# Zipformer block on one core: splitting the last 416-token chunk of the second batch into 256 and 160 tokens whose attention takes both pairs of heads in one exponential

## The chip, the core and the metric

One core of a Trainium2 chip. The metric is the device time of one execution in microseconds (us), the median of several runs. Timed runs take turns with runs of the kernel before on the same chip. "Ratio" always means the mean time of one kernel's fast runs over the mean time of the other's fast runs of the same rounds, so it is not quite the ratio of the medians quoted; intervals are 95%. Several chips were used, so times are compared within one job only.

## The reference, cut to what matters

Two sequences of 4000 tokens, width 144, four heads of 36, feed-forward width 576, everything in bf16.

```python
def reference(x, ...):
    x = x + 0.5 * silu(ln(x) @ w_ff1a) @ w_ff1b          # feed-forward 1
    q, k, v = split(ln(x) @ w_qkv)
    p = softmax(q @ k.T * Dh ** -0.5)                     # 4000 x 4000, per head and batch
    x = x + (p @ v) @ w_o
    a, b = split(ln(x) @ w_pw1)
    h = a * sigmoid(b)                                    # GLU
    x = x + silu(depthwise_conv5(h, dw)) @ w_pw2          # needs the two neighbour tokens on each side
    x = x + 0.5 * silu(ln(x) @ w_ff2a) @ w_ff2b           # feed-forward 2
    return ln(x)
```

## The kernel before

Python code generates the instructions one by one and orders them with a model of the engines' times (a list scheduler); each engine then runs its list in order. Each batch is cut into seven chunks of 512 tokens and one of 416: chunks 0 to 7 and 8 to 15.

```python
    CPB = -(-T // CH)                       # 8 chunks a batch, CH = 512
    def nc_(c):
        return min(CH, T - c % CPB * CH)    # 512, the last 416
```

Attention runs in groups: one chunk and one pair of heads. A group has 31 tiles of 128 keys; the last 32 keys are one more tile in the first group of each chunk, for all four heads. For a tile, TensorE makes the scores of both heads of the pair (four 64x64 pieces side by side), ScalarE takes one exponential over both (1024 columns, or 832 in the last chunk), TensorE multiplies by the values. VectorE computes the exponential of some tiles by a polynomial.

```python
    groups = [(b, qc, p) for b in range(Bsz) for qc in range(CPB) for p in range(2)]
    # cut
        for hh in range(2):                                          # emit_S: the scores of tile n
            bk = 2 * (n % 2) + hh
            s_mm(gi, kt, hh, PSV[:, bk, 0:m], [("ps", bk)], 0.0535)
    # cut
        exps[n] = op("act", "activation", PT[:, n % NPT, :, 0:m], PSV[:, s:s + 2, 0:m], ACT.Exp, ...)
```

When a chunk's attention is complete its remaining chain starts: epilogue (copy, transpose, normalise), output projection, LayerNorm, GLU, convolution (it also needs the next chunk's GLU), second feed-forward, LayerNorm, store. Each LayerNorm is done in two halves, by these instructions on VectorE and GpSimd ("POOL" in the profile):

```python
        for i in range(2):
            op("dve", "bn_stats", ST[0:n, u, i, :], X[...], ...)
        for i in range(2):
            op("dve", "bn_aggr", MV[0:n, u, i, :], ST[0:n, u, i, :], ...)
        op("pool", "tensor_scalar", RS[0:n, u, :, 1], MV[0:n, u, :, 1], LN_EPS, None, op0=ALU.add, ...)
        op("pool", "tensor_tensor", RS[0:n, u, :, 0], RS[0:n, u, :, 1], NHALF[0:n, :], op=ALU.pow, ...)
        rest = not (mode["front"] or mode["tail"])      # middle: GpSimd normalises and a DMA transposes
        # cut: normalisation on VectorE or GpSimd
```

The softmax here doesn't subtract the row's maximum and nothing guards it: scores larger than these inputs give would overflow.

Of the kernel before, what the change touches and what calls it, by code (L numbers as in the profile page):

```python
# [12 lines left out]
D = 144  # L13
H = 4
DH = 36
# [268 lines left out]
def bass_standalone__conformer_family_zipformer__speech_kernel(  # L284
# [15 lines left out]
    CPB = -(-T // CH)  # L300
    NCH = Bsz * CPB
    NBLK = NCH * NB
    NKT = T // KTL
    REM = T - NKT * KTL
    assert Dm == D and REM == 32 and (T % CH) % (2 * NB) == 0

    def nc_(c):
        return min(CH, T - c % CPB * CH)

# [3 lines left out]
    def t0(c):  # L313
        return c // CPB * T + c % CPB * CH

# [13 lines left out]
    NSER = 3  # L329
    NPRE = 2  # L330
# [29 lines left out]
    RD = sb("RD", [2, NB, 2], F32)  # L360
# [61 lines left out]
    for c in range(1, CPB):  # L422
        load_x("sp", c)

    def load_rest():
        load("sp", "w2", WO[0:HD, :, :], kh(w_o), ["WO"])
        load("sp", "w2", WP1[0:HD, :, 0:2 * D], kh(w_pw1), ["WP1"])
        load("sp", "w2", WP2[:, NB, :], w_pw2[0:128, :], [("WP2", 0)])
        for i in range(NB):
            op("sp", "dma_start", WP2[32 * i:32 * i + 16, i, :], w_pw2[128:D, :], q="w2", r=[("WP2", "0")],  # L430
               w=[("WP2", 1 + i)], cost=0.7)
        load("sp", "w2", DWR[0:KCONV, :], dw, ["DWR"])
        load_ff("sp", "w2", WA2, WB2, w_ff2a, w_ff2b, "W2")
        for c in range(CPB, NCH):
            load_x("sp", c)
# [117 lines left out]
    def is_flat(c):  # L553

        return c % CPB == CPB - 1

# [177 lines left out]
    def vrem(c, s):  # L734

        b = c // CPB
        r0 = nc_(c) - REM
        bk = yield need("pe", banks, dur=0.24)
        for h in range(H):
            for k in range(2):  # L740
                op("pe", "matmul", PSV[32 * h:32 * h + 32, bk, 0:DH], lhsT=XT[0:HD, s, k * CH + r0:k * CH + r0 + REM],
                   rhs=WQKV[0:HD, k, 2 * D + h * DH:2 * D + (h + 1) * DH], start=k == 0, stop=k == 1,
                   skip_group_check=True, r=[("XT", s, 0), ("XT", s, 1), "WQKV"], w=[("ps", bk)], cost=0.03, kind="r")
        yield need("dve")
        for h in range(H):
            op("dve", "tensor_copy", VR[32 * h:32 * h + 32, b, h, 0:DH], PSV[32 * h:32 * h + 32, bk, 0:DH],
               r=[("ps", bk), "VR0", "VR1"], w=[("VR", b)], cost=0.14)
        banks.give(bk)

    def krem(c):  # L750
        b = c // CPB
# [24 lines left out]
    def pre2(c):  # L776
# [4 lines left out]
        last = c % CPB == CPB - 1  # L781
        kids = S.spawn([proj(KT, WK, "WK", c, s, 0), proj(QT, WQ, "WQ", c, s, 0), vproj(c, s, 0), vproj(c, s, 1),
                        proj(KT, WK, "WK", c, s, 1), proj(QT, WQ, "WQ", c, s, 1)] + ([vrem(c, s)] if last else []))
# [37 lines left out]
    def post1(c, a):  # L821

        b, cc, n = c // CPB, c % CPB, tb(c)
# [18 lines left out]
        if cc == 0:  # L842
            op("pool", "memset", U[:, v, :, 0:1], 0.0, w=[("UL", v)], cost=0.1)
        else:
            op("pool", "tensor_copy", U[:, v, :, 0:1], U[:, w, :, KTL:KTL + 1],
               r=[("U", w)], w=[("UL", v)], cost=0.25)
            op("pool", "tensor_copy", U[:, w, :, KTL + 1:KTL + 2], U[:, v, :, 1:2],
               r=[("U", v)], w=[("UR", w)], cost=0.25)
        if cc == CPB - 1:
# [33 lines left out]
    def post2(c):  # L883
        b, cc, n = c // CPB, c % CPB, tb(c)
        last = cc == CPB - 1
# [33 lines left out]
    def epilogue(b, qc, p, gi):  # L919
        c = b * CPB + qc  # L920
        n, nt = nc_(c), tb(c)
        op("dve", "tensor_copy", OTA[:, 0:n], PSV[:, 4, 0:n], r=[("ps", 4)], w=["OTA"], cost=0.63)
        op("dve", "tensor_tensor", OTF[:, gi % 2, 0:n], PSV[:, 5, 0:n], OTA[:, 0:n], op=ALU.add,
           r=[("ps", 5), "OTA"], w=[("OTF", gi % 2)], cost=0.63)
        bk = yield need("pe", banks, dur=0.84)
        for i in range(NB):
            op("pe", "transpose", PSV[0:nt, bk, i * 128:(i + 1) * 128], OTF[:, gi % 2, i * nt:(i + 1) * nt],
               IDF[:, :], r=[("OTF", gi % 2), "IDF"], w=[("ps", bk)], cost=0.21, kind="f")
        if p == 0:
            an_of[c] = yield need("dve", anp)  # L930
        yield need("dve", cond=lambda: c in an_of)
        a = an_of[c]
        v = PSV[0:nt, bk, :].rearrange("p (i h d) -> p i h d", i=NB, h=2)
        op("dve", "reciprocal", RD[0:nt, gi % 2, :, :], v[:, :, :, DH], r=[("ps", bk)], w=[("RD", gi % 2)],
           cost=0.14)
        yield need("dve")
        op("dve", "tensor_tensor",
           AN[0:nt, a, :, p, 0:HD].rearrange("p i (h d) -> p i h d", h=2), v[:, :, :, 0:DH],
           RD[0:nt, gi % 2, :, :].rearrange("p i (h o) -> p i h o", o=1).to_broadcast([nt, NB, 2, DH]),
           op=ALU.mult, r=[("ps", bk), ("RD", gi % 2), "AN0"], w=[("AN", a)], cost=0.42)  # L940
        banks.give(bk)
        if p == 1:
            yield from post1(c, a)

    groups = [(b, qc, p) for b in range(Bsz) for qc in range(CPB) for p in range(2)]
    left = []
    for gi, g in enumerate(groups):
        kts = list(range(NKT))
        if g[2] == 0:
            kts.insert(1 if gi else NKT, NKT)  # L950
        left.append(kts)
    its = []
# [9 lines left out]
    def s_mm(gi, kt, hh, o, keys, cost):  # L962
        b, qc, p = groups[gi]
        c = b * CPB + qc
        k0 = b * T + kt * KTL
        for m0, m1 in halves:
            op("pe", "matmul", o[m0:m1, :], lhsT=KT[64 * hh:64 * hh + 64, p, k0 + m0:k0 + m1],
               rhs=QT[64 * hh:64 * hh + 64, p, q_at(c):q_at(c) + nc_(c)], start=True, stop=True, skip_group_check=True,
               r=[("WKT", b * CPB + kt // NB), ("WQT", c % NQ)], w=keys, cost=cost, kind="q")

    def emit_S(n):
        gi, kt = its[n]
        b, qc, p = groups[gi]
        c = b * CPB + qc
        m = nc_(c)
# [6 lines left out]
        for hh in range(2):  # L982
            bk = 2 * (n % 2) + hh
            s_mm(gi, kt, hh, PSV[:, bk, 0:m], [("ps", bk)], 0.0535)

    def emit_exp(n):
        gi, kt = its[n]
        b, qc, p = groups[gi]
        m = nc_(qc)
        s = 2 * (n % 2)  # L990
        if kt == NKT:
            exps[n] = op("act", "activation", PR[:, qc % 2, 0:m], PSV[:, s, 0:m], ACT.Exp, bias=0.5 * LN2, scale=ESCALE,
                         r=[("ps", s)], w=[("PR", qc % 2)], cost=0.05 + m * 0.000833)
            return
        exps[n] = op("act", "activation", PT[:, n % NPT, :, 0:m], PSV[:, s:s + 2, 0:m], ACT.Exp, bias=0.5 * LN2,
# [3 lines left out]
    def stolen():  # L999

        g0 = group()
        if g0 is None or g0 < 2:
            return None
        for gi in (g0, g0 + 1):
            if gi < len(groups) and len(left[gi]) >= LEAD:
                b, qc, p = groups[gi]
                if b * CPB + qc in kv_done and b * CPB + left[gi][-1] // NB in kv_done:
# [3 lines left out]
    def dve_exp():  # L1011
# [4 lines left out]
        while True:  # L1016
# [9 lines left out]
            b, qc, p = groups[gi]  # L1026
            m = nc_(qc)
            for hh in range(2):
                s_mm(gi, kt, hh, PSV[:, bks[hh], 0:m], [("ps", bks[hh])], 0.0535)
# [24 lines left out]
    def rem_O(gi, stop):  # L1054
        b, qc, p = groups[gi]
        m = nc_(qc)
        for hh in range(2):
            op("pe", "matmul", PSV[64 * hh:64 * hh + 64, 4, 0:m], lhsT=VR[:, b, 2 * p + hh, :],
               rhs=PR[:, qc % 2, 0:m], start=False, stop=stop, skip_group_check=True,
               r=[("PR", qc % 2), ("VR", b)], w=[("ps", 4)], cost=0.11, kind="c")  # L1060

    def o_mm(gi, kt, P, key):
        b, qc, p = groups[gi]
        m = nc_(qc)
        tile = (b * CPB + kt // NB) * NB + kt % NB
        for r, (m0, m1) in enumerate(halves):
            for hh in range(2):
                op("pe", "matmul", PSV[64 * hh:64 * hh + 64, 4 + r, 0:m], 
                   lhsT=VA[m0:m1, tile, VH * (2 * p + hh):VH * (2 * p + hh) + 64],
                   rhs=P[m0:m1, hh, 0:m], start=kt == 0, stop=False, skip_group_check=True,  # L1070
                   r=[key, ("VA", b * CPB + kt // NB)], w=[("ps", 4 + r)], cost=0.0535, kind="q")

    def emit_O(n):
# [3 lines left out]
        else:  # L1077
            o_mm(gi, kt, PT[:, n % NPT, :, :], ("PT", n % NPT))
            if kt == 0 and groups[gi][2] == 1:
# [3 lines left out]
    def o_out(gi):  # L1083
        o_left[gi] -= 1
        if o_left[gi] == 0:
            b, qc, p = groups[gi]
            if p == 1:
                att_done.add(b * CPB + qc)
            S.add(epilogue(*groups[gi], gi), first=True)

    def s_start(n):

        gi, kt = its[n]
        b, qc, p = groups[gi]
        kc = b * CPB + min(kt, NKT) // NB
        if kc not in kv_done:
            return None
        t = max(R.free["pe"], R.ready(("WKT", kc)), R.ready(("WQT", (b * CPB + qc) % NQ)))
        return max(t, exps[n - 2].done) if n >= 2 else t

    for c in range(CPB):
        S.add(ff1(c, True), ready=R.ready(("X", c, 0)))
    S.add(setup_qk(), ready=R.ready("WQKV"))
    for c in range(CPB):
        S.add(pre2(c))
    R.filler = filler
    while len(ff1_done) < CPB or 0 not in kv_done:
# [48 lines left out]
    while n_e < n_s or group() is not None:  # L1156
# [9 lines left out]
        lag = max(len(att_done) - len(fin), LAG - 1 + CPB + ((g0 or 0) + 1) * AHEAD - len(kv_done)  # L1166
# [5 lines left out]
        if th is not None and (stuck or a is None or t < a or (th.req[0] == "act" and t < a + 0.05)):  # L1172
# [3 lines left out]
            if mode["front"] and len(kv_done) == CPB:  # L1176
# [3 lines left out]
                for par in range(NPRE):  # L1180
                    S.add(series(g for c in range(CPB + par, NCH, NPRE) for g in (ff1(c, False), pre2(c))))
                for par in range(NSER):
                    S.add(series(post2(c) for c in range(par, NCH, NSER)))
# [58 lines left out]
```

## Time and profile before

| | |
|---|---|
| runs | 1052.78, 1029.52, 1033.81 us; median 1033.81 |
| profiled execution | span 1029.0 us, mean granted clock of TensorE 0.990 |
| last exponential ends | 989.6 us; tail behind it 39.4 us |

These are two 25 us stretches from the front of the trace of the kernel before. The columns are busy time (and instructions) of PE, PEld, DVE, ACT and POOL, then the granted clock, the DMA share and GB/s.

```profile
50.00:75.00 25.00, 23.28 (x206) 7.24 (x202) 17.06 (x70) 21.36 (x28) 7.44 (x16) 0.88 0.28 59
75.00:100.00 25.00, 20.97 (x247) 7.01 (x245) 15.95 (x68) 23.03 (x28) 5.89 (x11) 1.00 0.20 55
```

The clock is 0.88 in the first: from 49.1 us on TensorE ran at half clock for 6.8 us. The timeline of TensorE shows what lies before such a stretch:

```profile
49.16 0.64 PE L165 MATMUL PS<-QT,KT 64*64 64x512 bf16 x4 [1.07 <-ACT PT L165]
56.16 0.67 PE L165 MATMUL PS<-WQKV,XT 72*128 72x144 bf16 x8
56.76 0.41 PE L165 MATMUL PS<-QT,KT 64*64 64x512 bf16 x4
...
103.98 0.59 PE L165 MATMUL PS<-XT,WA 72*128 72x512 bf16 x2 [1.26 <-DMA XT<-XN]
```

TensorE is idle for 1.07 us ahead of 49.16. The same four score matmuls then take 0.64 us, and 0.41 again from 56.76 on. A second gap, of 1.26 us, lies ahead of 103.98. In this execution the clock came back quickly and the front cost little.

### The profile page before, as it was taken

To read this page: it belongs to the slowest core of one execution; us is meant where nothing else is said; L and a number is where in the kernel's file an instruction comes from. 1 tells how busy PE (TensorE), PEld (TensorE's weight loads), DVE (VectorE), ACT (ScalarE), POOL (GpSimd) and SP (SyncE) were. 2 spreads that over 40 slices of the span, in tenths; PEclk is the share of its full clock that TensorE was granted. 3 is DMA by queue.
4 is the path that set the end of the run, shared out by engine and by line. 5 is a ranking of instruction groups with operands and counts; after the bars stand their busy time and mean duration, and the time that the engine had idled before them with its cause. 6 is when DMAs were issued, how large, how long until landed. Compare 5 with 4: busy or idle time off the path is not lost.

```text
span 1029.0 us, 25199 instructions
## 1 busy us (share of the span) xinstructions
PE 871.0 (85%) x10488; PEld 321.4 (31%) x10488; DVE 749.9 (73%) x1938; ACT 963.6 (94%) x1202; POOL 369.7 (36%) x594
## 2 busy tenths in 40 slices
PE   9998898799889888788888888788888878788876
PEld 5532322233233323222323232222223223223335
DVE  8865467876657566887786676889877886886745
ACT  4789999999999999999999999999999999999963
POOL 5423260264547335041415353130425232313522
PEclk9999999999999999999999999999999999999997
DMA  3221120012112011020101110000001010101100
GB/s 95 51 64 42 24 43 2 17 32 38 32 22 42 11 28 25 2 30 4 30 7 25 22 26 17 14 14 11 18 17 31 9 23 11 22 12 25 21 15 14
DMA packets 89134, 25.43 MB, mean 25 GB/s; under 512 B 86444, under 2 KB 89020, under 8 KB 89020
## 3 DMA queue, kind: packets, MB, share of 16 engines
q1 hardware_dynamic: 87864, 23.35, 11.2%
q8 instruction: 82, 1.34, 0.5%
q10 hardware_dynamic: 1156, 0.47, 0.2%
q14 instruction: 32, 0.26, 0.1%
HBM read 3.31 MB, written 2.30 MB: 5 GB/s over the span
## 4 chain that ended last, share of the span: by engine, by line
ACT 67%; PE 25%; DVE 5%; issue 1%; POOL 1%; DMA 1%; POOLq 0%; DVEq 0%; ACTq 0%; SPq 0%
ACT PT L165 60%; PE PS L165 25%; ACT TH L165 6%; POOL RS L165 1%; ACT HT L165 1%; DVE HT L165 1%; DVE DF L165 1%; DVE PD L165 0%; DVE ST L165 0%; DVE DN L165 0%; DMA XT<-AN 0%; ACT KT L165 0%; DVE X L165 0%; DVE XN L165 0%; DVE DR L165 0%
## 5 line engine op out<-in xcount | busy, mean ns | idle before, releaser
L165 ACT ACTIVATE PT<-PS 128x1024 bf16<-128x1024 f32 (+1 forms) x927 | 870.5, 1066 | 10.6 <-PE PS L165 8.4
L165 PE MATMUL PS<-QT,KT 64*64 64x512 bf16 (+1 forms) x3968 | 403.4, 393 | 118.5 <-ACT PT L165 104.8
L165 PE MATMUL PS<-PT,VA 64*64 64x512 bf16 (+1 forms) x3708 | 360.1, 374 | 0.8 <-ACT PT L165 0.8
L165 PEld LDWEIGHTS PS<-QT,KT 64*64 64x64 bf16 x3968 | 115.5, 103 | 441.8 <-ACT PT L165 371.0
L165 POOL TENSOR_SCALAR RS<-MV 128x2 f32<-128x2 f32 (+1 forms) x160 | 37.8, 236 | 582.8 <-DVE MV L165 575.3
L165 POOL TENSOR_SCALAR XN<-X,MV,RS 128x144 bf16<-128x144 bf16 (+1 forms) x232 | 206.2, 901 | 6.8
L165 DVE SCALAR_TENSOR_TENSOR HT<-TH,PS 128x512 bf16<-128x512 bf16 (+3 forms) x110 | 67.7, 623 | 84.0 <-ACT TH L165 83.9
L165 POOL TENSOR_TENSOR RS<-RS,NHALF 128x2 f32<-128x2 f32 (+1 forms) x160 | 117.1, 732 | 13.3
L165 PEld LDWEIGHTS PS<-PT,VA 64*64 64x64 bf16 x3708 | 111.4, 106 | 20.5 <-issue 8.7
L165 ACT ACTIVATE TH<-PS 128x512 bf16<-128x512 f32 (+4 forms) x170 | 97.3, 573 | 6.0 <-PE PS L165 5.4
L165 PE MATMUL PS<-XT,WA 72*128 72x512 bf16 (+3 forms) x384 | 89.3, 348 | 13.1 <-DVE HT L165 9.6
L165 DVE TENSOR_SCALAR DN<-PS 128x512 bf16<-128x512 f32 (+1 forms) x130 | 87.3, 672 | 16.8 <-PE PS L165 10.3
L165 DVE TENSOR_TENSOR PD<-PD,DF 128x1024 f16<-128x1024 f16 (+1 forms) x130 | 88.5, 680 | 3.7
L165 DVE SCALAR_TENSOR_TENSOR DF<-PS,DN 128x512 f16<-128x512 f32 (+1 forms) x130 | 87.6, 674 | 4.1
L165 DVE BATCH_NORM_STATS2 ST<-X 128x6 f32<-128x144 bf16 (+1 forms) x320 | 81.5, 296 | 3.2
L165 DVE SCALAR_TENSOR_TENSOR X<-PS,X 128x288 bf16<-128x288 f32 (+1 forms) x128 | 57.2, 448 | 35.9 <-PE PS L165 35.6
L165 PE MATMUL PS<-WB,HT 128*128 128x144 bf16 (+1 forms) x640 | 50.3, 230 | 1.2 <-ACT HT L165 0.6
L165 PEld LDWEIGHTS PS<-XT,WA 72*128 72x128 bf16 x384 | 29.2, 99 | 67.6 <-DVE HT L165 28.2
L165 PEld LDWEIGHTS PS<-WB,HT 128*128 128x128 bf16 (+1 forms) x640 | 41.2, 104 | 19.2 <-issue 5.8
L165 DVE COPY OTA<-PS 128x512 f32<-128x512 f32 (+1 forms) x32 | 21.7, 679 | 32.9 <-PE PS L165 32.9
L165 DVE TENSOR_TENSOR PD<-PD,DN 128x1024 uint16<-128x1024 f16 (+1 forms) x65 | 44.4, 688 | 1.7
L165 DVE BATCH_NORM_AGGREGATE MV<-ST 128x2 f32<-128x6 f32 (+1 forms) x320 | 43.9, 168 | 0.0
(83 smaller groups left out, 596.0 us busy)
## 6 DMA issues: line engine op xcount, KB each, us to landing
X<-in_x_dram SPq DMA_DIRECT2D x14, 144.0 KB, 3.3
out_dram<-XN SPq DMA_DIRECT2D x28, 72.0 KB, 1.8
XT<-XN SPq DMA_TRANSPOSE x110, 2.4
XT<-AN SPq DMA_TRANSPOSE x30, 2.5
X<-in_x_dram SPq DMA_DIRECT2D x2, 117.0 KB
out_dram<-XN SPq DMA_DIRECT2D x4, 58.5 KB
WA<-in_w_ff1a_dram ACTq DMA_DIRECT2D x1, 144.0 KB
WB<-in_w_ff1b_dram ACTq DMA_DIRECT2D x1, 144.0 KB
```

Source lines behind the costliest of these rows:

```text
L165: ins = getattr(eng, o.name)(*o.a, **o.k)
```

## The change

The intent: the end of the kernel is a chain of the last chunk's steps, so make the last chunk small (160 tokens). To keep the number of exponentials, let a small chunk's exponential take both pairs of heads: 2 x 2 x 256 = 1024 and 2 x 2 x 160 = 640 columns. Further parts: a list of chunks in place of arithmetic, no VectorE tiles while more than three chunks await their end (`OPEN`), and queues that hand out the next chunk to whichever worker is free. The core of the diff (the renamings that follow from it are left out):

```diff
-    CPB = -(-T // CH)
+    chunks = []
+    for b in range(Bsz):
+        for t in range(0, T, CH):
+            n = min(CH, T - t)
+            parts = [n] if n == CH or b < Bsz - 1 else [2 * KTL, n - 2 * KTL]
+            for j, m in enumerate(parts):
+                chunks.append((b, t + sum(parts[:j]), m))
...
+    OPEN = 3
...
-        if g0 is None or g0 < 2:
+        if g0 is None or g0 < 2 or len(att_done) - len(fin) > OPEN:
...
-    groups = [(b, qc, p) for b in range(Bsz) for qc in range(CPB) for p in range(2)]
+    groups = []
+    for c in range(NCH):
+        groups += [(c, (0, 1))] if 2 * nc_(c) <= CH else [(c, (0,)), (c, (1,))]
...
+        for j, p in enumerate(ps):
+            for m0, m1 in halves:
+                op("pe", "matmul", o[m0:m1, j * n:(j + 1) * n], lhsT=KT[64 * hh:64 * hh + 64, p, k0 + m0:k0 + m1],
+                   rhs=QT[64 * hh:64 * hh + 64, p, q_at(c):q_at(c) + n], ...
...
-                for par in range(NSER):
-                    S.add(series(post2(c) for c in range(par, NCH, NSER)))
+                keys, posts = iter(range(C0, NCH)), iter(range(NCH))
+                for _ in range(NSER):
+                    S.add(series(post2(c) for c in posts))
```

After the change the last chunks are 13 and 14 (512 tokens), 15 (256) and 16 (160).

## The prediction

> **What bounds the kernel now.** I read the page first (shares, chain), then the busy time by stretch, the instruction groups by form between 100 and 989 us, and the chain and the timeline of the last 60 us.
>
> ```profile
> PE 871.0 (85%) x10488; PEld 321.4 (31%) x10488; DVE 749.9 (73%) x1938; ACT 963.6 (94%) x1202; POOL 369.7 (36%) x594
> PEclk9999999999999999999999999999999999999997
> ACT 67%; PE 25%; DVE 5%; issue 1%; POOL 1%; DMA 1%; POOLq 0%; DVEq 0%; ACTq 0%; SPq 0%
> ```
>
> ```profile
> 968.00:989.60 21.60, 17.76 (x232) 5.83 (x232) 8.02 (x22) 19.97 (x28) 5.25 (x8) 0.94 0.07 14
> 989.60:1029.00 39.40, 27.04 (x301) 20.75 (x301) 23.95 (x95) 12.86 (x26) 11.52 (x27) 0.87 0.05 12
> ```
>
> The columns after the length are PE, PEld, DVE, ACT, POOL, the granted clock, the DMA share and GB/s. There are two regimes. Until 989.6 us ScalarE is the bound: it runs the softmax exponentials nearly without a pause (99% busy in every hundred from 300 on). Then comes a tail of 39.4 us in which ScalarE is busy for 12.9 us and no engine is full: a chain of dependent steps of the last chunks (attention epilogue, GLU, convolution, second feed-forward, LayerNorm, store). The change aims at the tail: the last chunk, which alone is still missing its attention, becomes smaller.
>
> ```profile
> 699.76 10.09 ACT PT L165 x11
> 765.12 0.49 ACT TH L165
> 766.53 0.28 ACT TH L165
> ...
> 970.04 1.62 ACT L165 ACTIVATE PT<-PS 128x832 bf16<-128x832 f32 x2 [1.44 <-PE PS L165]
> 971.85 13.72 ACT L165 ACTIVATE PT<-PS 128x832 bf16<-128x832 f32 x18 [0.19 <-PE PS L165]
> ```
>
> The first three are from the chain, the others from the timeline. The pace of back-to-back exponentials is 10.09 / 11 = 0.917 us for 1024 columns and 13.72 / 18 = 0.762 us for 832: 0.81 ns a column, and by that 0.606 us for 640. A tanh costs 0.49 us for 512 columns, 0.28 for 256. The 1.44 us is what happens when TensorE has other work ahead of the scores: ScalarE waits.
>
> ```profile
> 1003.43 2.58 PE PS L165 x25
> 1010.65 0.52 ACT XT L165
> 1011.22 7.39 PE PS L165 x42
> 1018.63 2.06 ACT HT L165 x4
> 1021.03 0.81 PE PS L165 x10
> ```
>
> This is the chain at the end: 989.6 last exponential, 1000.6 GLU of the last chunk, 1003.4 convolution, 1011.2 second feed-forward of chunk 15 and behind it in TensorE's queue that of chunk 14, 1021.0 its last matmuls, 1029.0 end.
>
> **What the Trainium skill says.** "ScalarE: Activation LUTs", section "What ACT_TABLE_LOAD costs": an ACTIVATE takes a fixed part plus 0.833 ns a column, and neighbours overlap by about 93 ns. The trace agrees on the slope (0.81) and shows a smaller rest, about 0.08 us an instruction. So equal columns in equally many instructions cost the same, however they are cut. "TensorE: Matmul & The Clock Gate", section "Wait — 56ns, not 53.3ns?": starts of matmuls never follow closer than about 25 ns apart when alone; but this kernel runs four 64x64 pieces side by side, and the timeline shows 20 GLU matmuls in 1.28 us, 16 of them of 104 columns, so the small score matmuls (160 columns) should fit: I estimate 16 of them, four abreast, at 0.3 us of the 0.606 us that their exponential takes. "PSUM — Partial Sum Buffer", section "Engine vs sequencer instructions": matmuls start and complete in program order. The trace agrees (the 42 matmuls of two feed-forwards above run as one line), and my argument rests on it.
>
> **The change, part by part.** (1) Columns of attention. Before, chunk 15 has 416 tokens: two groups of 31 tiles, each exponential 2 x 416 = 832 wide. After, chunk 15 (256 tokens) takes both head pairs in one exponential of 1024 columns, chunk 16 (160 tokens) in one of 640. 62 x 832 = 31 x 1024 + 31 x 640: the same number of instructions and the same columns. Nothing is won there.
>
> (2) Tiles that VectorE takes over. The instruction order of the built kernels has 813 + 114 exponentials before and 843 + 57 + 29 after (1024, 832 and 640 wide): VectorE does 65 tiles before, 63 after, and smaller ones. Exponentials: +30 x 0.917 - 57 x 0.762 + 29 x 0.606 = +1.6 us of ScalarE.
>
> (3) Other work of ScalarE ahead of the last exponential: by the order, two tanh of 512 fewer (-0.98), four of 416 fewer (-1.64), one of 208 fewer (-0.24), four of 256 more (+1.12), four of 160 (+0.8), one each of 128 and 80 (+0.3), small exponentials +0.07: -0.6 us. So the last exponential should end 1.0 us later if the pauses stay as they are.
>
> (4) Pauses. In the 160-token stage one tile lasts 0.606 us. The timeline shows a score matmul of 416 taking 0.37 us from start to end and the next exponential starting only then; with 0.3 us of TensorE free per tile, any other piece put between (the order has the convolution of chunk 13, 20 output matmuls of a feed-forward, two rounds of fp32 transposes, four hidden tiles) of more than about 0.35 us holds ScalarE up. By 0.7 for the convolution (1.27 us in the tail's timeline), 0.4 for each of two transposes (0.65) and each of two output groups (0.8), 0.1 each for the rest: some 3 us, against 1.6 us seen in 968 to 989.6. Call it +1.5.
>
> (5) The tail, the disputed part. One would think it shrinks: 160 tokens instead of 416. But the order says that the tail takes on more. Before, after the last exponential come two whole second feed-forwards (chunks 14 and 15) and the rest of 13. After, ScalarE still has 8 x 512 hidden activations (chunks 13 and 14), the set of chunk 15 and that of 16: the columns are 512 + 512 + 256 + 160 = 1440 tokens against 928. And TensorE's order puts chunk 14's feed-forward ahead of chunk 16's convolution. I walk the chain with the durations seen before. Last exponential at 0; epilogue copies of 320 columns instead of 416, two transposes and two normalisations instead of one, with VectorE work of chunk 15 between: attention output at 5.0 (before: 993.1 - 989.6 = 3.5). Convolution of chunk 14 goes first; output projection at 6.8 (before 4.6). LayerNorm to GLU, which does not depend on the width (statistics 0.5, aggregate 0.3, POOL 0.24 + 0.73, normalise 0.54, twice over): 12.6 (before 11.0). GLU to the neighbour columns 2.1 (before 2.86): 14.7. Chunk 15's convolution and projection: 16.5. Chunk 14's feed-forward: 12 matmuls, activations, 20 output matmuls, 5.1: 21.6. Only then chunk 16's convolution, 1.2; its residual and LayerNorm, 5.4 (before 1011.2 - 1005.6 = 5.6): 28.2. Before, that point is at 21.6, and then two large feed-forwards follow (9.8 to the last output matmuls); after, two small ones, 4.2: 32.4. From the last output matmuls to the end 8.0, as before: 40.4, against 39.4.
>
> The gain of the small last chunk (9.8 - 4.2 = 5.6 us) is thus paid back by the queue ahead of its convolution (6.6 us). Sum: +1.0 +1.5 +1.0 = +3.5 us on a span of 1029.0. The profiled run took 1030.8 and the runs' median is 1033.8, with one at 1052.8; a typical run is some 1031, so the sum gives 1034.5. I go to 1033, because the walk takes waits in a row that may overlap, and somebody chose these settings for a reason.
>
> **The rivals.** (a) The tail shrinks as intended. For it: no engine is full in the tail, the granted clock of the last stretches is low (0.87 over the tail, and lower while the two large feed-forwards run), so smaller pieces that keep TensorE busy may run at full clock, and the extra feed-forward fills holes. Against it: the order on TensorE. It would make the tail 33 to 35 us and the time about 1026. (b) The new cap on VectorE's tiles (none while more than three chunks await their end) or the changed order of the post-processing shifts pauses in the middle. For it: the orders differ from the first third on. Against it: nearly the same number of tiles and ScalarE 99% busy. Plus or minus 3 us. (c) TensorE becomes the bound in the 160-token stage, as each score step is now eight matmuls and weight loads: if a group of four cost 0.15 us instead of 0.075, a tile would take 0.6 us of TensorE without anything else, and the stage would grow by 6 to 8 us, time about 1041. Against it: the small GLU matmuls above.
>
> **Range and chances.** The rivals reach from 1026 to 1041, and run noise adds 2 us: 1025 to 1042 holds 8 in 10. Two per cent is 20 us, half the whole tail; no mechanism here gives it, only an outlying set of runs. Faster 0.03, within 0.95, slower 0.02.
>
> **What would show it.** In the profile of the changed kernel: the exponentials of 640 columns pace at 0.60 to 0.63 us where nothing intervenes; the last one ends at 991 to 994 us; waits of ScalarE on TensorE in the last 20 us before that sum to 2 to 4 us; the tail is 38 to 42 us, and the chain in it passes through chunk 14's feed-forward before the 160-token convolution. A tail below 36 us would show step 5 wrong, and rival (a) right; a last exponential after 997 us would show (b) or (c).

## More of the kernel before

After the last exponential the scheduler is in its "tail". There TensorE gets dummy matmuls (`DUM` in the trace) in the gaps that the scheduler expects, to keep its clock up:

```python
            if self.filler is not None and gap > 0.3:
                self.fill(int((gap - 0.15) / 0.11), o, lane)
```

## The result, and the profile after

The kernel after took 1066.2 us (1066.2, 1068.59, 1060.2) against 1033.81. The ratio is 1.0314, interval 1.0234 to 1.0394: slower by over 2%. The prediction said 1033, range 1025 to 1042. All three runs count as fast, because a run is called slow only against the fastest run of its own kernel; their granted clocks were 0.953 to 0.966, that of the profiled run before 0.990.

From the page of the kernel after: busy times, the granted clock in 40 slices, the shares of the chain that ended last.

```profile
PE 908.5 (85%) x11113; PEld 344.3 (32%) x11113; DVE 751.6 (71%) x1992; ACT 971.0 (91%) x1222; POOL 387.4 (36%) x626
PEclk9955799999999999999999999999999999999998
ACT 60%; PE 27%; DVE 6%; POOL 3%; DMA 2%; issue 1%; POOLq 0%; DVEq 0%; SPq 0%
```

ScalarE's share of the chain fell from 67 to 60% and its work hardly grew (971.0 against 963.6). The clock line has a hole in its third to fifth slice that the kernel before does not have. The same two stretches as before:

```profile
50.00:75.00 25.00, 24.78 (x144) 6.98 (x148) 12.38 (x55) 16.03 (x20) 6.36 (x14) 0.50 0.16 32
75.00:100.00 25.00, 25.00 (x143) 6.74 (x136) 8.53 (x21) 14.04 (x17) 1.00 (x3) 0.50 0.29 73
```

From 75 to 100 us TensorE is 100% busy, at half clock, and gets through 143 matmuls instead of 247; ScalarE falls to 14.0 us of 25. Where the 35.4 us between the two profiled executions come from, read at events that both traces have:

| event | before | after | behind by |
|---|---|---|---|
| second exponential of a 32-key tile starts | 125.3 | 149.6 | 24.3 |
| third one starts | 184.7 | 210.5 | 25.8 |
| last exponential ends | 989.6 | 1019.4 | 29.8 |
| end | 1029.0 | 1064.4 | 35.4 |
| half clock before 150 / middle / tail, us | 6.8 / 3.4 / 10.5 | 75.1 / 6.8 / 9.0 | |

So 24 to 26 us arise in the front, 4 in the middle, 5.6 in the tail. But the two built kernels have the same instructions in the same order on TensorE for their first 3,273 matmuls of some 10,500, which is the first 345 us of the trace before. The other engines have the same order too for the first 200 us, except that the last chunk's input is loaded by two transfers in place of one, at 79 to 85 us, when the hole had already begun. What happens in the front cannot be the change's work.

The tail of the kernel after as a stretch, and lines from its timeline of TensorE:

```profile
1019.30:1064.40 45.10, 30.84 (x372) 23.64 (x372) 29.28 (x129) 15.10 (x41) 19.95 (x45) 0.90 0.08 20
```

```profile
1036.49 2.34 PE L165 MATMUL PS<-XT,WA 72*128 72x512 bf16 x12
...
1040.79 0.55 PE L165 MATMUL PS<-U,DG 128*128 128x160 bf16 x9
...
1046.97 0.31 PE L165 MATMUL PS<-IDENT,XN 40*72 40x40 bf16 x4 [2.36 <-DVE XN L165]
...
1049.15 2.80 PE L165 MATMUL PS<-XT,WA 72*128 72x256 bf16 x18
1051.88 2.58 PE L165 MATMUL PS<-WB,HT 128*40 128x144 bf16 x20
...
1055.79 1.44 PE L165 MATMUL PS<-WB,HT 128*64 128x144 bf16 x20 [0.19 <-ACT HT L165]
```

As predicted, chunk 14's feed-forward (1036.49) stands ahead of chunk 16's convolution (1040.79). Then TensorE waits 2.36 us for a LayerNorm on VectorE (1046.97), and the last two small feed-forwards start at half clock: 20 output matmuls of 40 rows take 2.58 us, those of 64 rows, back at full clock, 1.44. VectorE has 129 instructions in this tail, against 95 before.

### The profile page after: what moved, and what is told of

Read it like the earlier page. It is cut to its first block, busy times and chain, and to the rows that moved or that the text cites.

```text
span 1064.4 us, 26568 instructions
## 1 busy us (share of the span) xinstructions
PE 908.5 (85%) x11113; PEld 344.3 (32%) x11113; DVE 751.6 (71%) x1992; ACT 971.0 (91%) x1222; POOL 387.4 (36%) x626
## 3 DMA queue, kind: packets, MB, share of 16 engines
q1 hardware_dynamic: 89119, 23.61, 10.6%
## 4 chain that ended last, share of the span: by engine, by line
ACT 60%; PE 27%; DVE 6%; POOL 3%; DMA 2%; issue 1%; POOLq 0%; DVEq 0%; SPq 0%
ACT PT L165 53%; PE PS L165 27%; ACT TH L165 5%; POOL RS L165 2%; DMA XT<-AN 1%; POOL XN L165 1%; DVE PD L165 1%; DVE DF L165 1%; DVE DN L165 1%; ACT HT L165 1%; DVE ST L165 1%; DMA XT<-XN 1%; DVE X L165 0%; DVE XN L165 0%; DVE HT L165 0%
## 5 line engine op out<-in xcount | busy, mean ns | idle before, releaser
L165 ACT ACTIVATE PT<-PS 128x1024 bf16<-128x1024 f32 (+2 forms) x929 | 874.5, 1060 | 20.8 <-PE PS L165 18.1
L165 PE MATMUL PS<-QT,KT 64*64 64x512 bf16 (+3 forms) x4216 | 412.9, 387 | 118.6 <-ACT PT L165 101.5
L165 PE MATMUL PS<-PT,VA 64*64 64x512 bf16 (+3 forms) x3952 | 371.2, 371 | 0.5 <-ACT PT L165 0.5
L165 POOL TENSOR_SCALAR RS<-MV 128x2 f32<-128x2 f32 (+3 forms) x170 | 40.4, 238 | 588.5 <-DVE MV L165 588.3
L165 POOL TENSOR_SCALAR XN<-X,MV,RS 128x144 bf16<-128x144 bf16 (+3 forms) x242 | 214.4, 896 | 6.5
L165 POOL TENSOR_TENSOR RS<-RS,NHALF 128x2 f32<-128x2 f32 (+3 forms) x170 | 123.3, 725 | 14.2
L165 PE MATMUL PS<-XT,WA 72*128 72x512 bf16 (+5 forms) x408 | 92.2, 346 | 11.9 <-DVE HT L165 7.3
L165 ACT ACTIVATE TH<-PS 128x512 bf16<-128x512 f32 (+6 forms) x172 | 95.3, 555 | 7.3 <-PE PS L165 6.8
L165 DVE BATCH_NORM_STATS2 ST<-X 128x6 f32<-128x144 bf16 (+3 forms) x340 | 86.5, 296 | 3.3
L165 DVE TENSOR_TENSOR PD<-PD,DF 128x1024 f16<-128x1024 f16 (+2 forms) x126 | 86.1, 683 | 3.6
L165 DVE SCALAR_TENSOR_TENSOR DF<-PS,DN 128x512 f16<-128x512 f32 (+2 forms) x126 | 85.1, 676 | 3.9
```

The lines of the kernel that those rows point to most:

```text
L165: ins = getattr(eng, o.name)(*o.a, **o.k)
```

## The experiments

Two theories at the start. **Clock**: the front's half clock is chance and could hit either kernel; the change itself costs far less than 3%. **Change**: something in the new kernel (queues, cap, packed groups) causes it.

### 1. Both kernels again, and dummy matmuls to hold the clock

The first two are unchanged. The other two put dummy matmuls into the first 80 attention tiles of each kernel:

```diff
         for hh in range(2):
             bk = 2 * (n % 2) + hh
+            if n < NHOT:                       # 80
+                op("pe", "matmul", PSV[:, bk, 0:256], lhsT=DUM[:, 0:128], rhs=DUM[:, 0:256], ...)
             s_mm(...)
```

> The changed kernel itself, five rounds. Its first trace shows TensorE's clock at half from 48 to 110 us and again for 14 us, in a part of the program that is the same in both kernels; the kernel before has 7 us of that. Theory A (chance[...]): the five times scatter, with some near 1038 us and a mean clock near 0.99 and others near 1065 with a clock near 0.957. Theory B (something in the changed kernel makes the clock stay low): all five are 1058 to 1069 us with a clock of 0.95 to 0.967.

> The kernel before, as it stands. Theory A: one or two of its runs are at 1050 us or above with a clock of 0.96 or so, like the 1052.8 us on record. Theory B: all of them are at 1029 to 1036 us with a clock of 0.985 or more.

> The changed kernel with one added dummy matmul (128x128 weights, 256 columns, into the bank that is then overwritten) ahead of each score matmul pair of the first 80 tiles; the order of everything else is the same. If the low clock of the first 140 us is what costs 26 of the 35 us (time lag of the two traces at the second small exponential), the clock stays at 0.98 or more and the time is 1035 to 1043 us in every round. If the lag has another cause, it stays near 1065.

> The kernel before with the same dummy matmuls. If they cost little and keep the clock up: 1028 to 1034 us in every round, none at 1050. Against the changed kernel with the same dummies, which should then be 5 to 10 us longer: about 4 us lost in the middle and 5 us in the tail, by the two first traces.

Measured: the kernel after 1049.9 us (ratio 1.0115, 1.0054 to 1.0177), the kernel before, again, 1034.69 (0.9965, 0.9907 to 1.0023). In the new traces the front had 27.3 us of half clock in the kernel after and 20.5 in the kernel before; the second 32-key exponential came at 135.0 and 130.9. So the hole of 75 us did not come back, and the kernel before had one of its own. Theory B's figures (1058 us and more in every run) are out: four of the six runs lie at 1046 to 1053. Theory A's did not come exactly either: none lies near 1038. Executions that the record calls slow are left out of the ratios: one of six of the kernel after (1068.94), and in the same job one of six (1044.81) and three of eleven (1052.74 to 1061.54) of the kernel before. Half of the first result was chance; 1.5% (1.0115 over 0.9965) remains. Why all three runs of the first job were hit and only one of these six came as high is not shown.

The dummies were a bad instrument: 1132.6 and 1119.03 us, and 1089 to 1090 and 1070 to 1075 in the executions with a clock of 0.98 or more. Lines from the timeline of TensorE of r1_after_hot show why:

```profile
140.36 0.40 PE L165 MATMUL PS<-QT,KT 64*64 64x512 bf16 x2
140.69 0.28 PE L165 MATMUL PS<-DUM 128*128 128x256 bf16 x1
140.91 0.40 PE L165 MATMUL PS<-QT,KT 64*64 64x512 bf16 x2
```

A tile's four score matmuls, which ran side by side in 0.41 us, are now two and two with a dummy between: about 0.55 us for each pair and its dummy. Their forecasts (1035 to 1043 and 1028 to 1034) failed with that. As a measure of the change they are too disturbed, though the ratio of their fast runs, 1.0495 over 1.0335, is again 1.5%. One by-product: the kernel before, with dummies, three times took 1163 to 1165 us at a mean clock of 0.90, and the kernel after three times 1175 to 1184. The profile caught one of those; its clock line, with slices of 29 us:

```profile
PEclk9855555557999999999999999999999999999999
```

That run shows that the kernel before can sit at half clock for 200 us too.

### 2. Fill only the two gaps, then take the change apart

Ten dummy matmuls go into each of the two gaps shown above (before the third tile, and before the first feed-forward matmul of batch 1), in both kernels. The order on all engines is otherwise unchanged.

```diff
+        if n == 2:
+            for _ in range(10):
+                op("pe", "matmul", PSV[:, 4, 0:256], lhsT=DUM[:, 0:128], rhs=DUM[:, 0:256], ...)
...
+        if c == C0 and m == 0 and nm == "W1":          # c == CPB in the kernel before
+            for _ in range(10):
+                op("pe", "matmul", PSV[:, bk, 0:256], lhsT=DUM[:, 0:128], rhs=DUM[:, 0:256], ...)
```

r2_nosplit_fill is the filled kernel after without the split (`OPEN` and queues stay); r2_nogrp_fill keeps the split without the joint exponential (for which one small buffer, `RD`, is also made larger):

```diff
-            parts = [n] if n == CH or b < Bsz - 1 else [2 * KTL, n - 2 * KTL]
+            parts = [n]                                               # r2_nosplit_fill
...
-        groups += [(c, (0, 1))] if 2 * nc_(c) <= CH else [(c, (0,)), (c, (1,))]
+        groups += [(c, (0,)), (c, (1,))]                              # r2_nogrp_fill
```

> The kernel before with ten dummy matmuls (128x128 weights, 256 columns) at two places where TensorE stands idle: into the output bank before its first use, ahead of the third score pair; and into the first hidden bank of chunk 8's first feed-forward, ahead of its wait for a transposed input. No other instruction moves. In the traces of both kernels TensorE's clock falls to half just after these two gaps, with an occupancy of the array (rows x columns x time, worked out from the matmuls) of 0.27 to 0.38 of the 3.4 us before[...]. If the gaps set it off, the clock stays full through the first 140 us, the mean clock is 0.99 or more and all rounds lie between 1024 and 1032 us; if the cause is elsewhere, runs of 1035 to 1060 remain.

> The changed kernel with the same twenty dummies. If the low clock at the start was luck and nothing of the change: all rounds at 1036 to 1042 us, that is 9 to 13 us above the kernel before with dummies; of these about 3 to 5 us lie ahead of the last exponential and 6 to 8 in the tail. If the change itself costs 30 us, it stays above 1050.

> The changed kernel with the last chunk left whole (416 tokens in two groups), and with the cap on VectorE's tiles, the shared queues of post-processing and all else of the change kept, plus the dummies. Theory: the split is the whole of the cost, then 1025 to 1032 us, as the kernel before with dummies. Rival: the cap or the queues cost it, then 1036 us or more.

> The changed kernel with the split but each pair of heads in an exponential of its own (512 and 320 columns; four groups in place of two), plus the dummies. By columns and fixed part alone 60 more exponentials would cost 60 x 0.08 = 5 us. By the loop from an exponential to the next scores (0.37 us for a score matmul plus two hand-overs), which no longer fits into exponentials of 0.35 to 0.5 us, it costs some 20 us in the last two stages: 1055 to 1070 us.

| kernel | median (range), us | ratio to the kernel before (interval) | last exponential | tail | half clock: front / middle / tail |
|---|---|---|---|---|---|
| r2_before_fill | 1028.62 (1027.19 to 1032.64) | 0.9899 (0.9859 to 0.9940) | 988.2 | 39.4 | 0 / 6.8 / 10.6 |
| r2_after_fill | 1043.61 (1040.40 to 1047.92) | 1.0048 (1.0003 to 1.0092) | 990.4 | 48.2 | 0 / 0 / 21.6 |
| r2_nosplit_fill | 1031.61 (1028.09 to 1036.51) | 0.9919 (0.9876 to 0.9963) | 994.1 | 36.1 | 0 / 13.7 / 2.7 |
| r2_nogrp_fill | 1070.00 (1066.06 to 1074.14) | 1.0289 (1.0244 to 1.0333) | 1011.1 | 58.0 | 0 / 50.1 / 34.1 |

In the same job the unfilled kernel before ranged from 1032.91 to 1052.69. The two stretches once more, r2_before_fill:

```profile
50.00:75.00 25.00, 22.83 (x229) 7.49 (x228) 18.77 (x78) 23.28 (x31) 7.44 (x16) 1.00 0.31 65
75.00:100.00 25.00, 20.43 (x241) 6.80 (x243) 15.22 (x66) 23.25 (x29) 7.18 (x12) 1.00 0.18 52
```

What follows. (a) Twenty dummy matmuls in two gaps keep the front at full clock in all four traces, and in the ten of experiments 3 to 5, and take the wide spread away; the gaps are what sets the half clock off. Both gaps were filled at once, so what each does alone is not shown. (b) With the front equal, the change still costs 15.0 us (1.0048 over 0.9899 is 1.5%, the figure of the repeated kernels). In the profiled executions it is 11.0 us: 2.2 up to the last exponential and 8.8 in the tail. (The profiled one is the fastest of its kernel's six, so some 4 of the 15 us stand in no trace; the forecast for this kernel was 1036 to 1042, its median 1043.6.) (c) Without the split 3 us remain, with intervals that overlap: what the cap and the queues cost is not resolved; 12 of the 15 us go with the split, with intervals apart (1.0048 and 0.9919). (d) The joint exponential is a good idea within it: without it 26 us more. How much of this is the exponentials and how much the clock (50 us of half clock in the middle, 34 in the tail) is not separated.

The chain that ended last in r2_after_fill shows how its tail begins and ends:

```profile
986.43 4.99 POOL XN L165 x6
991.45 3.12 DMA XT<-XN
994.71 6.00 PE PS L165 x32
...
1020.56 8.58 PE PS L165 x65
```

Chunk 13's LayerNorm is still done the way of the middle: GpSimd normalises (six instructions in 4.99 us), a DMA transposes (3.12 us), and TensorE, in program order, stands still for it with chunk 16's chain behind. At the end a piece of 8.58 us, transposes and the two small feed-forwards, runs mostly at half clock.

### 3. Take these two terms out

"late": VectorE normalises and TensorE transposes already during the last group, so GpSimd and DMA drop out of the start of the tail. "dense": twice as many fillers in the tail, against the half clock. All kernels are filled as in 2.

```diff
+        if g0 is None or g0 >= len(groups) - 1:
+            mode["late"] = True
...
-        rest = not (mode["front"] or mode["tail"])
+        rest = not (mode["front"] or mode["tail"] or mode["late"])    # late
...
-                self.fill(int((gap - 0.15) / 0.11), o, lane)
+                self.fill(int((gap - 0.15) / self.dens), o, lane)     # dense: 0.06 in the tail, else 0.11
```

> The changed kernel with dummies, and from the start of the last attention group on VectorE (0.3 us each) in place of GpSimd (0.9 us each) normalises. In the trace of the changed kernel with dummies TensorE waits 1.8 us after the last exponential for a transposed input whose six normalisations took GpSimd 5.0 us, and the work behind it starts 3 us later than the prediction's walk had it. Theory: that queue is a term of the tail; it then starts chunk 13's first hidden tile within 2 us of the last exponential in place of 4.3, and the tail goes from 48.2 to 43 to 46 us. Rival: other queues are as long; the wait moves and the tail stays at 47 to 50 us.

> The changed kernel with dummies, and in the tail about twice as many filler matmuls in the same gaps (all else in the same order). In the tail of the changed kernel with dummies the clock is at half for 21.6 of 48.2 us, in the kernel before with dummies for 10.6 of 39.4; the last two small feed-forwards took 8.6 us in which the walk had 4.2. Theory: the low clock costs about a quarter to a half of its length; the half-clock time falls below 10 us and the tail to 42 to 45 us. Rival: the fillers hold up the chain; the tail is as long or longer.

> Both together. If the two terms are apart from each other the tail is 39 to 42 us and the time 1031 to 1036: the split then still gains nothing over the whole chunk. If it falls below the kernel before with dummies (1027 to 1033 us), the split was right and only the tail's waits were wrong.

> The kernel before with dummies and with the denser fillers in the tail. Its tail has 10.6 us at half clock, among them the two large feed-forwards. If the denser fillers hold the clock: the tail goes from 39.4 to 36 or 37 us and the time to 1023 to 1028 us, the best version. If they do not, 1027 to 1033 as before.

| kernel | median (range), us | ratio (interval) | tail | half clock in the tail |
|---|---|---|---|---|
| r3_after_late | 1042.84 (1040.10 to 1046.27) | 1.0090 (1.0054 to 1.0126) | 46.4 | 19.5 |
| r3_after_dense | 1044.05 (1041.15 to 1048.09) | 1.0095 (1.0056 to 1.0134) | 47.1 | 7.1 |
| r3_after_late_dense | 1037.74 (1035.61 to 1040.16) | 1.0039 (1.0003 to 1.0075) | 42.9 | 4.9 |
| r3_before_dense | 1029.86 (1027.39 to 1031.31) | 0.9961 (0.9927 to 0.9995) | 37.2 | 4.1 |

Each alone shortens the tail by only 1.1 to 1.8 us, no more than two traces of one kernel differ (42.9 here and 44.6 in experiment 4); both together by 5.3, and their runs are 5 to 6 us faster than with either alone. All four forecasts were missed by a little. Each edit did its own part: with "late" chunk 13's feed-forward starts 0.8 us after the last exponential in place of 4.3, and with "dense" the half clock in the tail fell from 21.6 to 7.1 us. So neither of the two terms alone was what made the tail long. The profiled executions of the first two also had 23.9 us of half clock in the middle, so their spans are not compared, only their tails. With both terms out, the tail of the split is still 42.9 us against 37.2 for the kernel before, which got the denser fillers but not "late".

### 4. The rest of the tail: GpSimd's part of the LayerNorm?

The tail after the split holds 18 LayerNorm halves, before it 12, and a half takes about as long for 40 rows as for 128. Was that the rest? The first cut of work takes GpSimd's two instructions out of every half in the tail, in both kernels, which gives a wrong result (relative error 0.04):

```diff
-        op("pool", "tensor_scalar", RS[0:n, u, :, 1], MV[0:n, u, :, 1], LN_EPS, None, ...)
-        op("pool", "tensor_tensor", RS[0:n, u, :, 0], RS[0:n, u, :, 1], NHALF[0:n, :], op=ALU.pow, ...)
+        if not mode["tail"]:
+            (the same two)
```

> Control, the same kernel as r3_after_late_dense: split, front filled, VectorE normalising during the last group, fillers in the tail twice as dense. Both theories: about 1036 to 1040 us, its tail in the trace 42 to 44 us.

> Control, the same kernel as r3_before_dense. Both theories: 1028 to 1032 us, its tail 36.5 to 38 us. The difference of the tails is to come out again at 5 to 6.5 us.

> As r4_after_ld, but in the tail GpSimd's two instructions of each LayerNorm half (0.24 + 0.73 us: the addition of eps and the power -0.5) are left out, so that the normalisation uses an old factor: a wrong result on purpose. Theory (the rest of the tail's growth is the number of LayerNorm half-steps that stand in a row, which do not get shorter with fewer tokens; the split has 18 halves in the tail where before has 12): the tail falls from 43 to 36 to 37.5, that is by 5.5 to 7, and by 2 to 4 more than the kernel before does. Rival (the rest is matmuls queued ahead on TensorE and the clock): it falls by the same as before does, some 3 to 4 us, to 39 to 40.

> As r4_before_d, with the same two GpSimd instructions of each LayerNorm half left out in the tail: a wrong result on purpose. Both theories: the tail falls by 3 to 4 us, from 37.2 to some 33.5. Theory: the two tails then differ by 2 to 4 us; rival: still by 5 to 6.5.

| kernel | median (range), us | tail | fell by |
|---|---|---|---|
| r4_after_ld (r3_after_late_dense again) | 1038.38 (1034.11 to 1041.73) | 44.6 | |
| r4_before_d (r3_before_dense again) | 1030.50 (1025.72 to 1031.30) | 37.2 | |
| r4_after_nors | 1036.31 (1035.06 to 1039.50) | 41.5 | 3.1 |
| r4_before_nors | 1025.25 (1024.21 to 1027.06) | 33.9 | 3.3 |

Both fall alike; the distance stays at 7.4 and 7.6. My theory in this form falls. (The scheduler reacts to such a cut, so the order of instructions in the tail also changes a little, here and in experiment 5.) The timeline of VectorE of r4_after_ld tells why it could:

```profile
1014.63 0.55 DVE L165 TENSOR_SCALAR XN<-X,MV,RS 128x144 bf16<-128x144 bf16 x2 [0.24 <-POOL RS L165]
1015.09 0.24 DVE L165 BATCH_NORM_AGGREGATE MV<-ST 128x2 f32<-128x6 f32 x2
1015.25 0.42 DVE L165 SCALAR_TENSOR_TENSOR X<-PS,X 64x288 bf16<-64x288 f32 x1
1015.70 0.51 DVE L165 BATCH_NORM_STATS2 ST<-X 64x6 f32<-64x144 bf16 x2
1016.47 0.54 DVE L165 TENSOR_SCALAR XN<-X,MV,RS 128x144 bf16<-128x144 bf16 x2 [0.26 <-POOL RS L165]
```

The halves stand in single file, one every 1.84 us, but VectorE waits for GpSimd only 0.24 to 0.26 us of it. The rest is VectorE's own work, and 64 rows cost as much as 128.

### 5. VectorE's part of the LayerNorm

The same cut for VectorE's statistics (bn_stats, bn_aggr) in the tail; GpSimd stays and waits for the residual instead. Wrong again (relative error 0.07).

> As r4_after_ld, but in the tail VectorE's statistics of each LayerNorm half (two bn_stats, 0.50 us together, and two aggregates, 0.23) are left out, GpSimd's two instructions stay and now wait for the residual itself: a wrong result on purpose. Theory A (the rest of the tail's growth is VectorE's own work on the LayerNorm halves, which stand in single file: r4_after_ld shows one half every 1.83 us between 1014.6 and 1020.1, of which VectorE waits only 0.23 to 0.27 for GpSimd; 18 halves in the tail against 12): the tail falls from 44.6 to 35 to 38, and comes within 2 to 4.5 us of that of the kernel before with the same cut. Theory B (the order on TensorE, whatever VectorE does): it falls by 3 to 4.5 us, as the kernel before does, and keeps its distance of about 7.

> As r4_before_d, with the same four VectorE instructions of each LayerNorm half left out in the tail: a wrong result on purpose. Both theories: the tail falls from 37.2 to 32.5 to 34.5. Theory A: the two tails then differ by 2 to 4.5 us; B: by 6 to 8.

Measured: 1031.87 us (1027.16 to 1037.48) and 1026.90 (1022.98 to 1028.20). The tails as stretches: of the controls r4_after_ld and r4_before_d, and of the two cut kernels.

```profile
992.30:1036.90 44.60, 34.06 (x456) 26.85 (x456) 30.88 (x136) 14.44 (x40) 17.17 (x40) 0.94 0.07 16
```

```profile
992.30:1029.50 37.20, 28.71 (x390) 23.51 (x390) 23.71 (x95) 12.45 (x27) 11.51 (x27) 0.95 0.06 13
```

```profile
995.70:1032.00 36.30, 29.96 (x362) 23.25 (x362) 20.25 (x66) 14.72 (x38) 17.02 (x40) 0.91 0.08 19
```

```profile
994.10:1026.10 32.00, 25.68 (x332) 20.28 (x332) 16.96 (x49) 11.32 (x24) 11.38 (x27) 0.95 0.06 15
```

The split's tail falls by 8.4 us (44.6 to 36.2), the other by 5.2 (37.2 to 32.0), and the distance from 7.4 to 4.2. That is what theory A expected for the distance (2 to 4.5); the tail before fell by half a microsecond more than expected. So VectorE's LayerNorm work carries some 3 us of the difference by these traces, or 1.5 if the control's other trace (42.9) is taken. The 4.2 that remain are not settled. The split's trace had 6.8 us of half clock in its tail there against 3.0, and the residuals and normalisations of six more halves are still in, but no run separates these; and one profiled execution of each kernel stands behind the tails (the control moved from 42.9 to 44.6 between two jobs).

## Why the prediction was wrong, point by point

**The first 1.6% was the clock, and the failed step is "run noise adds 2 us".** Half of the measured 3.1% was a hole in the granted clock where both kernels run the same instructions. The prediction gave "only an outlying set of runs" a chance of 2% for crossing the line, although one of the three runs of before stood at 1052.8. Taking that run at its word would have given a range that reaches some 20 us higher. The Trainium skill, "TensorE: Matmul & The Clock Gate", section "What's actually happening", describes a gate that is halved after an idle window of about 3.4 us and released after a busy one. The trace agrees on the grid: half-clock stretches are whole multiples of 3.413 us (6.8, 13.65, 61.4). It does not agree on the conditions: idle gaps of 1.1 and 1.3 us, a third of a window, came before the falls, and being busy did not release the clock, for TensorE was 100% busy at 0.50 for 25 us. What does release it stays open. By an estimate from the traces of the two kernels and their repeats (rows x columns of each matmul for as long as its columns stream: 0.43 us for 512 columns at half clock, half of that at full) the array was 23 to 34% full in the 3.4 us before each fall in the front and 70 to 88% before each return there. But windows at 74 and 75% brought no return, and in two tails the clock came back after 35 and 39%, so no threshold comes out of these traces.

**Steps 1 to 3 (equal columns, ScalarE +1.0) and step 4 (pauses +1.5): the sum came out, partly by luck.** With the clock equal the last exponential ends 2.2 us later (988.2 to 990.4); predicted was 2.5. But up to there ScalarE is busy for 950.4 us in r2_before_fill and 952.4 in r2_after_fill, 1.9 more in place of 1.0, and pauses for 37.8 and 38.0, 0.3 more in place of 1.5: two misses that offset each other. The pace of the 640-column exponentials, from the timeline of ScalarE of the kernel after, and the last of its waits:

```profile
1007.37 6.34 ACT L165 ACTIVATE PT<-PS 128x640 bf16<-128x640 f32 x10
...
1017.31 2.12 ACT L165 ACTIVATE PT<-PS 128x640 bf16<-128x640 f32 x3 [0.45 <-PE PS L165]
```

This is 0.63 us each (predicted 0.60 to 0.63). ScalarE's waits on TensorE from 999 us on are 0.34, 0.18 and 0.45: 1.0 us, where 2 to 4 were predicted and r2_before_fill has 1.5. So rival (c), TensorE as the bound, did not come. In the first profile the last exponential came at 1019.4, beyond the 997 that was to show rival (b) or (c); it was neither, but the front. A detail: by the prediction's own numbers an exponential's rest beside its columns is 0.09 us (0.917 - 0.81 x 1.024), not 0.08. Nothing rests on it.

**Step 5 (the tail), the other step that failed: the queue on TensorE was right, the terms behind it were mis-sized.** From the last exponential, in us:

| point of the walk | predicted | kernel after (first profile) | r2_after_fill |
|---|---|---|---|
| attention output | 5.0 | 6.2 | 8.2 |
| output projection | 6.8 | 7.3 | 9.9 |
| GLU of chunk 16 | 12.6 | 13.1 | 15.7 |
| convolution of chunk 15 | 14.7 | 15.1 | 17.7 |
| chunk 14's feed-forward ends | 21.6 | 21.6 | 24.2 |
| last small feed-forwards start | 28.2 | 29.8 | 32.4 |
| last output matmuls start | 32.4 | 36.4 | 39.1 |
| end | 40.4 | 45.0 | 48.2 |

Down to chunk 14's feed-forward the walk is right within 1.2 us in the first profile. "A convolution of 1.2, its residual and LayerNorm 5.4" took 8.2 us from there: chunk 16's LayerNorm stands in one file with chunk 14's last LayerNorm and chunk 15's halves on VectorE, a queue that the walk left out here since it followed TensorE's. "Two small ones, 4.2" took 6.6, counted as in the prediction to the start of the last output matmuls: TensorE had just waited 2.36 us, and they ran mostly at half clock. The last piece, 8.0, took 8.6. How much of this is the half clock is not separated: in experiment 3 two thirds of it went and the tail shortened by 1.1 us. Rival (a) rested on the opposite, that small pieces would keep the clock up. In r2_after_fill the first two points are 3.1 to 3.2 us late as well: TensorE waits 1.8 us for the DMA of chunk 13 (1.6 in the first profile), which the walk did not have, and the convolution of chunk 14 runs at half clock (2.34 us instead of 1.27). Predicted growth of the tail +1.0; measured +5.6 and +8.8.

**Size of the change itself.** With the front's clock held, +15 us in the runs, 1.5%, where the sum said +3.5: outside the range (1043.6 against 1042) by little, inside "within 2%". **Rival (b)** (cap and queues, plus or minus 3 us): 3 us, not resolved.

**A better version.** The best is the kernel before with the two gaps filled: r2_before_fill, 1028.62 us and ratio 0.9899, with runs from 1027 to 1033 where the unfilled kernel of the same job ranged from 1033 to 1053. The split does not reach it, even mended (1037.7 to 1038.4).

## What to carry to other kernels

Before explaining a difference, look where in time it arises; if the two programs are the same up to there, it is not the change, and the clock line is the first suspect. A smaller last chunk saves only what scales with its tokens: count the steps that do not (LayerNorm halves, instruction starts, waits) on every engine of the chain, not only on the one whose order you know. In a stretch of small dependent pieces TensorE can lose its clock, so cost its matmuls there at half clock as well, and put a few dummy matmuls into known gaps, never between matmuls that are meant to run side by side.

## What the Trainium skill lacked or had wrong

- "TensorE: Matmul & The Clock Gate", "What's actually happening": the table lets one busy window of about 3.4 us restore the clock. Here TensorE was 100% busy from 75 to 100 us, by the profile's count, at a granted clock of 0.50. What restores it stays open.
- The same page, "HAM oscillation — how this bites in real kernels", gives the rule as no idle gaps of TensorE over about 3.4 us (the section after it also blames frequent short idles, without a length). Here two gaps of 1.07 and 1.26 us were enough, and ten dummy matmuls in each kept the front at full clock.
- "What's actually happening" puts the warm-up ramp at under 1% of a span; it has no figure for a later fall. Here half clock in the front put one profiled execution 24 to 26 us behind another of the same instructions, over 2% of 1030, and the kernel before alone ranged from 1029 to 1062 us in one job, slow executions included.
- I found no page that says what a dummy matmul costs inside a group that runs side by side: a 256-column one between two pairs of 64x64 matmuls turned 0.41 us into about 1.1 us a tile.
- I found no page with the length of a LayerNorm half as a unit: one every 1.84 us in the tail, with 64 rows as dear as 128 (0.42 + 0.51 + 0.23 + 0.54 us on VectorE).
